# The first head of a fused attention block by halves from two queues, with the second head's work in another order

## The chip, the cores and the metric

The kernel runs on one core of one Trainium2 chip. The metric is the device time of one execution in microseconds (us). The core has five engines with a queue of instructions each: TensorE (PE, with weight loads shown apart as PEld), VectorE (DVE), ScalarE (ACT), GpSimd (POOL) and SyncE (SP, which issues most of the transfers). A transfer is issued by an engine's queue and carried out by 16 DMA engines.

## The reference, cut to what matters

Three layers follow one another: attention restricted to buckets, a gated layer, and a layer that mixes by Fourier transforms and ends in two matmuls. The change touches the start of the first.

```python
# batch 2, 8 heads, 768 positions, head size 64, 6 bits
q_bits = (q @ proj > 0); k_bits = (k @ proj > 0)          # proj: 64 x 6
mask = bucket(q_bits)[:, None] == bucket(k_bits)[None, :]
scores = where(mask, q @ k.T / 8, -1e9)
attn = softmax(scores);  x = attn @ v                     # heads side by side: 2 x 768 x 512
x = sigmoid(conv(x)) * (x @ w_val) @ w_out                # causal convolution of 5 taps
u = x + real(fft2(x));  out = u + relu(layernorm(u) @ w_ch1) @ w_ch2
```

## The kernel before

All products run as float32r matmuls on numbers cut in two: a high part (`ht`, a copy rounded on its way out) and a low part (`lt`, what is left). The attention goes over 8 pairs of heads (`p`), a head `j` in each pair, and 6 tiles of 128 queries in each head: 96 tiles `n`. The order of instructions on each engine is the order in which the program writes them.

For a head, q and k are loaded side by side into `rqk` (`load`, L321), transposed on TensorE so that head size lies on partitions (q on 0 to 63, k on 64 to 127), and copied out as `ht` (ScalarE) and `lt` (VectorE). The bits come from a matmul with proj (`project_alone`, L445) and a sign (`L504`, `L509` for the first head, `start_bits` L535 for the second). Scores are two matmuls deep (`scores`, L549): the operand tiles `qk` (`q2`, `k2`) hold in their first half high and low parts, and in their second half the bits on partitions 0 to 6 (with a large weight, so that different buckets drive a score out of the softmax), and more low and high parts on 64 to 127. For the very first head these tiles are filled by copies of ScalarE and GpSimd in `start` (L460); for every later head by six transfers of SP (`qk_place`, L407) and two for the bits (`bits_place`, L431).

A tile then runs through `clamp` (L568, VectorE: reads the scores, leaves `sd` and the row's extreme), `expo` (L575, ScalarE), transposes (`ptp`, L593), a high copy (L601, ScalarE), a low copy (L605, VectorE) and the product with v (L616, TensorE). In the loop over `n` the scores and the clamp of tile n+3 stand beside the transposes of tile n. One bank pair (`pss`) holds the scores of the loop, so the scores of a tile wait for the clamp of the tile before; the pool `pst` has two buffers and holds the transposes.

`start` runs before the loop: first head, its bits, scores of tiles 0 to 2, second head's transposes and parts. In the first turns of the loop come the second head's bits (L538, then `bits_scale` on GpSimd, L458, then `bits_place`), loads of the convolution weights (`cwr`, L747, whose first use is VectorE's L146 in turn 2), and the transposes of the second pair (`qk_transpose`, L392), for which `load(1, 0)` and `load(1, 1)` have been issued by `start`.

Until the first data are there, TensorE runs matmuls on zeros (`idle`, L353; `WARM` counts them).

Of the kernel before, what the change touches and what calls it, by code (L numbers as in the profile page):

```python
# [10 lines left out]
F32 = mybir.dt.float32  # L11
# [23 lines left out]
WARM = (18, 3, 4)  # L35
# [48 lines left out]
def col_table():  # L84

    c = np.zeros((P, 6), np.float32)
    c[:64, 0] = 1.0
    c[64:, 0] = KSCALE
    c[:, 2] = -1.0
    c[0, 2] = 1.0  # L90
    c[:, 3] = -8.0 * 896 * 2.0 ** 20
    c[:, 4] = -8.0 * 897 * 2.0 ** 20

    for j in (0, NR):
        c[j : j + NB, 1] = 1.0
        c[j : j + NB, 5] = -0.5
        c[j + NB, 5] = 1.0
        c[j + 32 : j + 32 + NB, 1] = -2.0 * BIG
        c[j + 32 : j + 32 + NB, 5] = BIG
        c[j + 32 + NB, 5] = 3.0 * BIG  # L100
    return c
# [3 lines left out]
def block_kernel(  # L105
# [6 lines left out]
    def f32(ap):  # L112
        return ap.bitcast(F32)
# [7 lines left out]
    warm = cpool.tile([P, 1], F32, name="warm")  # L121
    nc.vector.memset(warm, 0.0)

# [178 lines left out]
    def attention(es):  # L302
# [24 lines left out]

        def load_v(p):
# [13 lines left out]

        ph = ap1.tile([P, 2, P], F32R, name="ph")
# [5 lines left out]

        zeros = ap0.tile([P, R, QB], F32R, tag="pth", name="zeros")[:, 0, :]  # L350
        nc.gpsimd.memset(f32(zeros), 0.0)
# [30 lines left out]
        nc.gpsimd.tensor_scalar(pr[64:128, :], pr[64:128, :], -1.0, 0.0, op0=ALU.mult, op1=ALU.add)  # L382
        project_parts(0)
# [8 lines left out]
        def qk_transpose(p, j, a):  # L392
# [11 lines left out]
            nc.scalar.activation(ht, tp, AF.Copy, scale=col[:, 0:1])  # L404
            nc.vector.scalar_tensor_tensor(lt, tp, col[:, 0:1], f32(ht), op0=ALU.mult, op1=ALU.subtract)
# [54 lines left out]
        def start():  # L460
# [7 lines left out]
            def turned(j, tps):  # L468
                for a in range(2):
                    for r in range(3):  # L470
                        nc.tensor.transpose(
                            tps[a][:, r * P : (r + 1) * P], rqk[:, j, 3 * a + r].rearrange("p i d -> p (i d)"), ident
                        )

            def high(j, tps):
                for a in range(2):
                    nc.scalar.activation(halves(st[0]["ht", j])[a], tps[a], AF.Copy, scale=col[:, 0:1])

            def low(j, tps):
                for a in range(2):  # L480
                    nc.vector.scalar_tensor_tensor(
                        halves(st[0]["lt", j])[a], tps[a], col[:, 0:1], f32(halves(st[0]["ht", j])[a]),
                        op0=ALU.mult, op1=ALU.subtract,
                    )

            first = two_banks()
            turned(0, first)
            idle(WARM[1])
            high(0, first)
            low(0, first)  # L490
            q1, q2_ = slice(0, HS), slice(HS, S)
            nc.scalar.copy(k2[0][0:64, 0, :], h[64:128, :])
            pool_copy(k2[0][64:128, 0, :], h[64:128, :])
            nc.scalar.copy(q2[0][0:64, 0, q1], h[0:64, q1])
            nc.scalar.copy(q2[0][64:128, 1, q1], h[0:64, q1])
            pool_copy(k2[0][64:128, 1, :], l[64:128, :])
            pool_copy(q2[0][64:128, 0, q1], l[0:64, q1])
            whole = pst.tile([P, 2, 512], F32, tag="t", name="bp")
            for a in range(2):
                project_alone(0, a, whole[0:64, a, :HS])  # L500
            bits = st[0]["bits"] = ap1.tile([P, S], F32R, tag="bits", name="bits")
            ks, qs = slice(32, 32 + NR), slice(0, NR)
            for a in range(2):
                nc.vector.tensor_scalar(halves(bits)[a][ks], whole[ks, a, :HS], 0.0, None, op0=ALU.is_gt)  # L504
# [929 lines left out]
```

## Time and profile before

| | |
|---|---|
| time, median of 3 runs | 617.6 us (616.6 to 618.74) |
| the profiled execution | 618.49 us, its span 616.7 us |
| TensorE busy | 603.8 us (98% of the span) |
| VectorE busy | 444.7 us (72%) |
| ScalarE busy | 358.6 us (58%) |
| GpSimd busy | 269.1 us (44%) |
| transfers | 62.02 MB, 101 GB/s over the span |

The span runs from the first to the last recorded instruction; the execution's own time has 1.79 us around it. Busy TensorE is no measure of how near it is to its peak, since its matmuls overlap and their ends are modelled. Of the 616.7 us the attention takes the first 250 or so; the change lies in the first 20.

### The profile page before, as it was taken

How to read it: one execution, taken by the hardware profiler on the slowest of the kernel's cores; microseconds unless marked ns; L12 is line 12 of the kernel's file. 1: busy time of each engine (PE TensorE's matmuls, PEld its weight loads, DVE VectorE, ACT ScalarE, POOL GpSimd, SP SyncE). 2: the span in 40 equal slices, each digit the busy share in tenths (PEclk: the TensorE clock that was granted, in tenths of full speed). 3: DMA queues.
4: the chain of work that ended last, by engine and by line, in shares of the span. 5: the costliest groups of instructions: out<-in, count | busy, mean ns of one | idle time of the engine just before them, and what ended most of it. 6: DMA issues, size and time to landing. Idle time of an engine off the chain costs nothing.

```text
span 616.7 us, 10435 instructions
## 1 busy us (share of the span) xinstructions
PE 603.8 (98%) x3711; PEld 539.2 (87%) x3711; DVE 444.7 (72%) x850; ACT 358.6 (58%) x712; POOL 269.1 (44%) x303
## 2 busy tenths in 40 slices
PE   8999999999999999999999999999999999999997
PEld 6889999999899989998899988888888888888886
DVE  5999999999899998799769788888885411111113
ACT  5988899988899887844625355555665111111121
POOL 8252488877788898792350633233231000000000
PEclk9999999999999999999999999999999999999999
DMA  6957585857566640162110243443440200000002
GB/s 141 224 127 172 130 182 147 180 150 157 151 156 166 191 120 14 61 243 70 36 35 0 70 132 118 126 136 109 133 136 1 103 0 1 2 0 1 0 1 102
DMA packets 54957, 62.02 MB, mean 101 GB/s; under 512 B 29184, under 2 KB 42664, under 8 KB 54650
## 3 DMA queue, kind: packets, MB, share of 16 engines
q1 hardware_dynamic: 54170, 57.81, 35.6%
q0 software_dynamic: 432, 3.55, 1.5%
q8 instruction: 29, 0.48, 0.3%
q14 instruction: 22, 0.18, 0.1%
q10 hardware_dynamic: 304, 0.01, 0.0%
HBM read 36.73 MB, written 3.19 MB: 65 GB/s over the span
## 4 chain that ended last, share of the span: by engine, by line
PE 72%; DVE 14%; ACT 3%; DMA 3%; issue 3%; POOL 2%; SPq 2%; ACTq 0%; POOLq 0%; DVEq 0%
PE pf L1341 20%; PE acc L1351 20%; PE sp L557 7%; PE op L616 6%; PE ptp L593 5%; DVE sd L568 3%; PE ps L1158 3%; DVE ptl L605 3%; PE ps L222 3%; PE ps L1222 2%; DMA qk<-ht 2%; PE late L222 1%; PE early L222 1%; PE bp L443 1%; DMA xs<-xc 1%
## 5 line engine op out<-in xcount | busy, mean ns | idle before, releaser
L1351 PE MATMUL acc<-w,hid 128*128 128x512 f32 x576 | 137.7, 391 | 0.0
L1351 PEld LDWEIGHTS acc<-w,hid 128*128 128x128 f32 x576 | 105.8, 188 | 20.3
L1344 DVE SCALAR_TENSOR_TENSOR hid<-pf,hid 128x512 fp32r<-128x512 f32 (+1 forms) x62 | 33.4, 556 | 120.4 <-ACT hid L1343 120.4
L1341 PE MATMUL pf<-uth,w 128*128 128x512 f32 (+1 forms) x496 | 96.8, 337 | 0.1
L568 DVE TENSOR_SCALAR_CACHE_REDUCE sd<-sp 128x768 f32<-128x768 f32 x96 | 91.1, 950 | 7.7 <-PE sp L557 7.2
L605 DVE TENSOR_TENSOR ptl<-ptp,pth 128x768 fp32r<-128x768 f32 x96 | 91.5, 953 | 5.9 <-ACT pth L601 3.8
L1343 ACT ACTIVATE hid<-pf 128x512 fp32r<-128x512 f32 (+1 forms) x62 | 28.9, 488 | 115.0 <-PE pf L1341 115.0
L557 PE MATMUL sp<-qk 128*128 128x512 f32 (+1 forms) x384 | 91.4, 360 | 4.3 <-DVE sd L568 3.2
L1341 PEld LDWEIGHTS pf<-uth,w 128*128 128x128 f32 x496 | 79.8, 189 | 13.8 <-DVE hid L1344 1.4
L575 ACT ACTIVATE sd<-sd,nm 128x768 f32<-128x768 f32 x96 | 90.1, 939 | 1.5 <-DVE sd L568 1.5
L601 ACT CAST pth<-ptp 128x768 fp32r<-128x768 f32 x96 | 77.1, 803 | 17.7 <-PE ptp L693 8.9
L162 POOL TENSOR_TENSOR w<-cv 128x512 fp32r<-128x512 f32 x31 | 40.1, 1294 | 88.8 <-DVE cv L157 80.3
L593 PE MATMUL ptp<-ident,sd 128*128 128x128 f32 x576 | 78.5, 272 | 0.2 <-ACT sd L575 0.2
L616 PE MATMUL op<-pth,v 128*128 128x256 f32 x288 | 74.1, 283 | 1.6 <-ACT xc L629 1.6
L616 PE MATMUL op<-ptl,v 128*128 128x256 f32 x288 | 73.8, 286 | 0.0
L557 PEld LDWEIGHTS sp<-qk 128*128 128x128 f32 x384 | 58.2, 189 | 13.8 <-DVE sd L568 7.4
L593 PEld LDWEIGHTS ptp<-ident,sd 128*128 128x128 f32 x576 | 65.8, 140 | 1.1 <-ACT sd L575 0.5
L616 PEld LDWEIGHTS op<-pth,v 128*128 128x128 f32 x288 | 54.2, 188 | 6.6 <-ACT xc L629 2.7
L634 POOL TENSOR_TENSOR xm<-xc,xs 64x256 f32<-64x256 f32 x48 | 35.2, 733 | 56.4 <-DMA xs<-xc 39.0
L616 PEld LDWEIGHTS op<-ptl,v 128*128 128x128 f32 x288 | 54.2, 188 | 0.3
L1341 PE MATMUL pf<-utl,w 128*128 128x512 f32 (+1 forms) x248 | 53.1, 336 | 0.0
L149 ACT ACTIVATE cv<-cv,col 128x512 int32<-128x512 int32 x32 | 23.2, 725 | 41.5 <-DVE cv L146 41.5
(214 smaller groups left out, 998.4 us busy)
## 6 DMA issues: line engine op xcount, KB each, us to landing
raw<-in_moe_w_ch_dram SPq DMA_DIRECT2D x32, 512.0 KB
qk<-ht SPq DMA_DIRECT2D x60, 192.0 KB
qk<-lt SPq DMA_DIRECT2D x30, 192.0 KB
rqk<-in_q_dram SPq DMA_DIRECT2D x16, 192.0 KB
rqk<-in_k_dram SPq DMA_DIRECT2D x16, 192.0 KB
rv<-in_v_dram SPq DMA_DIRECT2D x8, 384.0 KB
out_dram<-o SPq DMA_DIRECT2D x12, 256.0 KB
xs<-xc SPq DMA_DIRECT2D x47, 64.0 KB
```

Source lines behind the costliest of these rows:

```text
L162: nc.gpsimd.tensor_tensor(dst()[1], fold(g.bitcast(F32)), fold(e.bitcast(F32)), op=ALU.mult)
L557: nc.tensor.matmul(sp[:, cs], q2[i][:, m, qi * P : (qi + 1) * P], k2[i][:, m, cs], start=m == order[0], stop=m == order[1])
L568: nc.vector.tensor_scalar(sd[n], sp, CLAMP, None, op0=ALU.min, op1=ALU.min, accum_out=st[p]["nm"][:, n % 12 : n % 12 + 1],)
L575: nc.scalar.activation(sd[n], sd[n], AF.Exp, bias=st[p]["nm"][:, i : i + 1], scale=-1.0, accum_out=st[p]["sums"][:, i : i + 1],)
L593: nc.tensor.transpose(tp[:, r // 3, c0 : c0 + P], sd[n][:, r * P : (r + 1) * P], ident)
L601: nc.scalar.copy(p_parts(n)[0], tp)
L605: nc.vector.tensor_tensor(lo, tp, f32(ho), op=ALU.subtract)
L616: nc.tensor.matmul(po[kb], v3[:, r, c0 : c0 + P], pt[kb][x][:, r, :], start=r == 0 and x == 0, stop=r == R - 1 and x == 1,)
L634: add[kb] = lambda: nc.gpsimd.tensor_tensor(st[p]["xm"][mr, blk * QB : (blk + 1) * QB], xc[mr, :], xs[mr, :], op=ALU.add)
L1341: nc.tensor.matmul(pf, w[:, c, :], x[:, c, cs], start=n == 0, stop=n == 3 * NC - 1)
L1344: nc.vector.scalar_tensor_tensor(hl[:, cs], pf, 0.0, f32(hh)[:, cs], op0=ALU.max, op1=ALU.subtract)
L1351: nc.tensor.matmul(acc, x[:, ts_], w, start=f == 0 and n == 0, stop=f == NF - 1 and n == 2)
```

## The change

Loads. The first head's q and k come in halves of three rows each, q by SP's queue and k by ScalarE's. The two copies of proj go one by each queue, behind the halves. Warm-up matmuls: 13 for 18. The scale of the high and low parts is no column of the loaded table `col` any more, but a tile that VectorE sets.

proj's parts for the first head (`ph`, `pl`, `plus`) are made by VectorE, but for `plus`; GpSimd made them before. The first head's transposes, high and low parts go by halves. k's bits are written by VectorE straight into the operand tile, with scale and offset in one instruction, and q's go through `bits` and a ScalarE instruction (before, it was the other way round); rows of the table are exchanged for that. q's operands are filled for the first 128 columns first, then for the others of that half, then for the second half. The second head's transposes use the two banks of the first head's, not a tile of `pst`; three tiles of `pst` are then in use in the opening (two for the first head's bits, one for the scores of tile 1). The second head's high copies stand ahead of the first exponentials on ScalarE, and its low parts behind the clamp of tile 1 on VectorE. SP places the second head and its bits ahead of `load(1, 1)`.

```diff
-WARM = (18, 3, 4)
+WARM = (13, 3, 4)
...
+    nc.vector.memset(turn_scale[:64], 1.0)
+    nc.vector.memset(turn_scale[64:], KSCALE)
...
+        def load_halves():
+
+            t = st[0]["rqk"] = ap4.tile([P, 2, R, 2, D], F32, tag="rqk", name="rqk", bufs=2)
+            for a in range(2):
+                rs = slice(3 * a, 3 * a + 3)
+                for i, (eng, src) in enumerate(((nc.sync, q), (nc.scalar, k))):
+                    eng.dma_start(t[:, 0, rs, i, :], src[0, 0].rearrange("(p r) d -> p r d", r=R)[:, rs, :])
...
-        load(0, 0)
+        load_halves()
 
         pr = ap1.tile([P, NB], F32, name="pr")
-        for r in (0, 64):
-            nc.scalar.dma_start(pr[r : r + 64, :], proj)
+        nc.scalar.dma_start(pr[0:64, :], proj)
+        nc.sync.dma_start(pr[64:128, :], proj)
         nc.scalar.dma_start(col, t_col)
         load(0, 1)
...
-        nc.gpsimd.tensor_scalar(pr[64:128, :], pr[64:128, :], -1.0, 0.0, op0=ALU.mult, op1=ALU.add)
-        project_parts(0)
+        nc.vector.tensor_scalar(pr[64:128, :], pr[64:128, :], -1.0, None, op0=ALU.mult)
+        spots = [(slice(64 * x, 64 * x + 64), 32 * x) for x in range(2)]
+        for rs, c0 in spots:
+            nc.vector.tensor_copy(ph[rs, 0, c0 : c0 + NB], pr[rs, :])
+        for rs, c0 in spots:
+            hd = f32(ph)[rs, 0, c0 : c0 + NB]
+            nc.vector.tensor_tensor(ph[rs, 0, 64 + c0 : 64 + c0 + NB], hd, pr[rs, :], op=ALU.subtract)
+            nc.gpsimd.tensor_tensor(plus[rs, 0, c0 : c0 + NB], pr[rs, :], hd, op=ALU.subtract)
+        for rs, c0 in spots:
+            nc.vector.tensor_copy(pl[rs, 0, c0 : c0 + NB], f32(ph)[rs, 0, c0 : c0 + NB])
...
+            for a in range(2):
+                turned(0, banks_[a], a)
             idle(WARM[1])
+            for a in range(2):
+                high(0, banks_[a], a)
+                low(0, banks_[a], a)
+                pool_copy(halves(k2_[64:128, 0, :])[a], halves(h[64:128, :])[a])
+            tile0 = slice(0, P)
+            nc.scalar.copy(k2_[0:64, 0, :], h[64:128, :])
+            nc.scalar.copy(q2_[0:64, 0, tile0], h[0:64, tile0])
+            nc.scalar.copy(q2_[64:128, 1, tile0], h[0:64, tile0])
+            pool_copy(q2_[64:128, 0, tile0], l[0:64, tile0])
+            pool_copy(k2_[64:128, 1, :], l[64:128, :])
+            bps = [pst.tile([P, 2, 512], F32, tag="t", name="bp")[:, 0, :HS] for _ in range(2)]
...
+            k_bits(0)
+            q_bits(0, 0, P)
+            k_bits(1)
+            q_bits(0, P, HS)
+            second = two_banks()
             load_v(0)
             load(1, 0)
+            for a in range(2):
+                turned(1, second[a], a)
             idle(WARM[2])
+            high(1, second[0], 0)
+            q_scaled(0, P)
+            high(1, second[1], 1)
+            sp = [scores(0, order=(0, 1))]
+            q_scaled(P, HS)
+            q_rest(P, HS)
+            clamp(0, sp[0])
+            q_bits(1, 0, HS)
+            sp.append(scores(1, pst.tile([P, 2, 512], F32, tag="t", name="sp")))
+            expo(0)
+            clamp(1, sp[1])
+            q_scaled(HS, S)
+            for a in range(2):
+                low(1, second[a], a)
+            q_rest(HS, S)
             project_parts(1)
-            sp = [scores(0, order=(0, 1)), scores(1, pst.tile([P, 2, 512], F32, tag="t", name="sp"))]
-            clamp(0, sp[0])
-            expo(0)
-            low(1, second)
-            clamp(1, sp[1])
             sp = scores(2)
+            qk_place(0, 1)
             values(0, 0)
-            qk_place(0, 1)
-            load(1, 1)
             expo(1)
             clamp(2, sp)
...
             bits_scale(bits)
             bits_place(0, 1)
+            load(1, 1)
```

On VectorE, from the first low parts to the fourth clamp, stood before (`lt` low parts, `bits` and `qk` the bits, `sd` a clamp):

```order
L481 SCALAR_TENSOR_TENSOR lt<-bp,col,ht 128x384 x2
L504 TENSOR_SCALAR bits<-bp 7x384 x2
L509 TENSOR_SCALAR qk<-bp,col 7x384 x2
L568 TENSOR_SCALAR sd,nm<-sp 128x768
L481 SCALAR_TENSOR_TENSOR lt<-tp,col,ht 128x384 x2
L568 TENSOR_SCALAR sd,nm<-sp 128x768 x2
L538 TENSOR_SCALAR bits<-bp 64x384 x2
L568 TENSOR_SCALAR sd,nm<-sp 128x768
```

The same stretch of VectorE's queue in the changed kernel, begun three rows earlier so that the last of proj's small operations are seen:

```order
L396 TENSOR_TENSOR ph<-ph,pr 64x6 x2
L399 CAST pl<-ph 64x6 x2
L492 SCALAR_TENSOR_TENSOR lt<-bp,turn_scale,ht 128x384 x2
L519 TENSOR_SCALAR qk<-bp,col 7x384
L524 TENSOR_SCALAR bits<-bp 7x128
L519 TENSOR_SCALAR qk<-bp,col 7x384
L524 TENSOR_SCALAR bits<-bp 7x256
L604 TENSOR_SCALAR sd,nm<-sp 128x768
L524 TENSOR_SCALAR bits<-bp 7x384
L604 TENSOR_SCALAR sd,nm<-sp 128x768
L492 SCALAR_TENSOR_TENSOR lt<-bp,turn_scale,ht 128x384 x2
L604 TENSOR_SCALAR sd,nm<-sp 128x768
```

proj's operations stand ahead of the first low parts, the bits are in five pieces of which one stands between the clamps of tiles 0 and 1, and the second head's low parts moved from ahead of tile 1's clamp to behind it.

On ScalarE, from the first high copies to the second exponential, stood before (`ht` high copies, `qk` copies into the operand tiles and the scaling of bits, `sd` the exponentials):

```order
L477 ACTIVATE ht<-bp,col 128x384 x2
L492 CAST qk<-ht 64x768
L494 CAST qk<-ht 64x384
L495 CAST qk<-ht 64x384
L505 ACTIVATE qk<-bits,col 7x768
L477 ACTIVATE ht<-tp,col 128x384 x2
L575 ACTIVATE sd,sums<-sd,nm 128x768 x2
```

and stands now:

```order
L489 ACTIVATE ht<-bp,turn_scale 128x384 x2
L507 CAST qk<-ht 64x768
L508 CAST qk<-ht 64x128
L509 CAST qk<-ht 64x128
L489 ACTIVATE ht<-bp,turn_scale 128x384
L529 ACTIVATE qk<-bits,col 7x128
L489 ACTIVATE ht<-bp,turn_scale 128x384
L529 ACTIVATE qk<-bits,col 7x256
L611 ACTIVATE sd,sums<-sd,nm 128x768
L529 ACTIVATE qk<-bits,col 7x384
```

The second head's high copies moved in between the pieces of the scaling, ahead of the first exponential.

On SP, from the last placement of the second head to the loads of the loop's first turn, stood before (numbers tell tiles apart; `rqk_211` is the second pair's q and k):

```order
L416 DMA qk_155<-lt_172 64x768
L326 DMA rqk_211<-in_q_dram 128x6x64
L326 DMA rqk_211<-in_k_dram 128x6x64
L435 DMA qk_153<-bits_202 7x768
L435 DMA qk_155<-bits_202 7x768
L747 DMA cwr_299<-in_moe_conv_w_dram 20x128
L775 DMA wvr_301<-in_moe_w_val_dram 128x256
```

and stands now (the second pair's tile is `rqk_213` there):

```order
L432 DMA qk_155<-lt_172 64x768
L451 DMA qk_153<-bits_204 7x768
L451 DMA qk_155<-bits_204 7x768
L327 DMA rqk_213<-in_q_dram 128x6x64
L327 DMA rqk_213<-in_k_dram 128x6x64
L783 DMA cwr_308<-in_moe_conv_w_dram 20x128
L811 DMA wvr_310<-in_moe_w_val_dram 128x256
```

The load of the second pair's second head changed places with the bits; `cwr` stands behind it in both.

## Rows read from the trace of the kernel before

**Rows 1.** Busy time by stage: span of stretch, engines' busy us, PEclk, DMA, GB/s.

```profile
40.00:100.00 60.00, 59.17 (x445) 55.55 (x445) 57.19 (x109) 53.75 (x111) 32.74 (x39) 1.00 0.67 158
```

**Rows 2.** The same view of VectorE alone, from 21.2 to 37.2.

```profile
21.20:37.20 16.00, 15.73 (x35) 1.00 0.72 169
```

**Rows 3.** The chain that ended last, to 40 us: start, us, what.

```profile
9.46 1.14 DVE qk L509 x2
...
10.60 0.63 PE sp L557 x2
...
11.25 0.98 DVE sd L568 x2
...
16.08 0.98 DVE sd L568 x2
...
17.10 0.98 PE sp L557 x4
```

**Rows 4.** Timeline to 17 us: start, us, engine, line, what, idle time before it.

```profile
2.63 1.28 ACT L341 ACT_TABLE_LOAD   x1 [2.63 <-issue]
...
4.68 0.21 POOL L382 TENSOR_SCALAR pr<-pr 64x6 f32<-64x6 f32 x1 [0.30 <-DMA pr<-in_proj_dram]
...
5.58 0.64 PEld L471 LDWEIGHTS bp<-ident,rqk 128*128 128x128 f32 x6 [0.20 <-issue]
...
6.16 1.05 ACT L477 ACTIVATE ht<-bp,col 128x384 fp32r<-128x384 f32 x2 [2.04 <-PE bp L471]
...
7.25 0.83 ACT L492 CAST qk<-ht 64x768 fp32r<-64x768 f32 x1
...
8.63 0.51 ACT L495 CAST qk<-ht 64x384 fp32r<-64x384 f32 x1
...
9.52 1.03 ACT L505 ACTIVATE qk<-bits,col 7x768 fp32r<-7x768 f32 x1 [0.38 <-DVE bits L504]
...
12.13 1.14 DVE L481 SCALAR_TENSOR_TENSOR lt<-tp,col,ht 128x384 fp32r<-128x384 f32 x2
...
13.19 0.95 DVE L568 TENSOR_SCALAR_CACHE_REDUCE sd<-sp 128x768 f32<-128x768 f32 x1
...
14.94 1.01 DVE L538 TENSOR_SCALAR bits<-bp 64x384 fp32r<-64x384 f32 x2
...
16.12 0.97 POOL L458 TENSOR_SCALAR bits<-bits,col 64x768 fp32r<-64x768 f32 x1 [0.72 <-ACT pth L601]
```

**Rows 5.** The same view of SP's queue, issues to 20 us.

```profile
0.76 0.69 SPq L326 DMA_DIRECT2D rqk<-in_q_dram  x1
...
15.54 0.86 SPq L326 DMA_DIRECT2D rqk<-in_q_dram  x1
...
17.24 1.72 SPq L435 DMA_DIRECT2D qk<-bits  x2
19.00 0.45 SPq L747 DMA_DIRECT2D cwr<-in_moe_conv_w_dram  x1
```

**Rows 6.** DMA queues from 2 to 4.3 us: packets, MB, share of 16 engines.

```profile
q1 hardware_dynamic: 1595, 0.40, 77.0%
```

**Rows 7.** Busy time by stage in the opening; columns as in rows 1.

```profile
2.40:3.00 0.60, 0.60 (x5) 0.60 (x5) 0.00 (x0) 0.37 (x1) 0.60 (x2) 1.00 0.54 126
3.00:3.60 0.60, 0.60 (x5) 0.60 (x5) 0.00 (x0) 0.60 (x1) 0.60 (x2) 1.00 1.13 241
```

**Rows 8.** Timeline from 22 to 24 us; columns as in rows 4.

```profile
22.65 0.20 DVE L146 TENSOR_SCALAR conv_tmp<-cwr 20x128 int32<-20x128 int32 x1
...
23.31 0.49 PE L399 MATMUL tp<-ident,rqk 128*128 128x128 f32 x3
```

**Rows 9.** DMA queues from 12 to 20.1 us; columns as in rows 6.

```profile
q1 hardware_dynamic: 2069, 1.62, 95.0%
```

**Rows 10.** The tile of the warm-up matmuls, 1.7 to 4.8: ns min, median, max.

```profile
L356 PEld LDWEIGHTS idle<-zeros x15: 286/330/333, 1.7 to 4.7; 128*128 128x128 f32 x15
```

**Rows 11.** The same tile from 5.05 to 9.6 us.

```profile
L356 PEld LDWEIGHTS idle<-zeros x10: 188/190/267, 4.9 to 9.1; 128*128 128x128 f32 x10
```

More of the change, by code (lines that the diff above doesn't have):

```diff
@@ L86, in col_table @@
     c = np.zeros((P, 6), np.float32)
-    c[:64, 0] = 1.0
-    c[64:, 0] = KSCALE
     c[:, 2] = -1.0
@@ L466, in start @@
             h, l = f32(st[0]["ht", 0]), f32(st[0]["lt", 0])
[L468 to L487, printed above, removed]
-            idle(WARM[1])
[L489 to L498, printed above, removed]
-            for a in range(2):
-                project_alone(0, a, whole[0:64, a, :HS])
+            def turned(j, tp, a):
+                for r in range(3):
+                    nc.tensor.transpose(tp[:, r * P : (r + 1) * P], rqk[:, j, 3 * a + r].rearrange("p i d -> p (i d)"), ident)
@@ new lines, in high, with low @@
+            def high(j, tp, a):
+                nc.scalar.activation(halves(st[0]["ht", j])[a], tp, AF.Copy, scale=turn_scale)
+            def low(j, tp, a):
+                nc.vector.scalar_tensor_tensor(
+                    halves(st[0]["lt", j])[a], tp, turn_scale, f32(halves(st[0]["ht", j])[a]),
+                    op0=ALU.mult, op1=ALU.subtract,
+                )
+            q2_, k2_ = q2[0], k2[0]
+            banks_ = two_banks()
+            for a in range(2):
+                turned(0, banks_[a], a)
@@ L501, in start @@
+            pool_copy(k2_[64:128, 1, :], l[64:128, :])
+            bps = [pst.tile([P, 2, 512], F32, tag="t", name="bp")[:, 0, :HS] for _ in range(2)]
+            for a in range(2):
+                project_alone(0, a, bps[a][0:64])
             bits = st[0]["bits"] = ap1.tile([P, S], F32R, tag="bits", name="bits")
             ks, qs = slice(32, 32 + NR), slice(0, NR)
-            for a in range(2):
-                nc.vector.tensor_scalar(halves(bits)[a][ks], whole[ks, a, :HS], 0.0, None, op0=ALU.is_gt)
@@ L505, in start, with k_bits @@
-            nc.scalar.activation(
-                k2[0][0:NR, 1, :], f32(bits)[ks], AF.Identity, scale=col[ks, 1:2], bias=col[ks, 5:6]
-            )
-            for a in range(2):
+            def k_bits(a):
                 nc.vector.tensor_scalar(
-                    halves(q2[0][0:NR, 1, :])[a], whole[qs, a, :HS], 0.0, col[qs, 5:6], op0=ALU.is_gt, op1=ALU.add
+                    halves(k2_[0:NR, 1, :])[a], bps[a][ks], 0.0, col[ks, 5:6], op0=ALU.is_gt, op1=ALU.add
                 )
-            second = pst.tile([P, 2, 512], F32, tag="t", name="tp")
@@ L513, in start, with q_bits, q_scaled, q_rest @@
-            second = [second[:, a, :HS] for a in range(2)]
+            def q_bits(a, c0, c1):
+                nc.vector.tensor_scalar(
+                    bits[qs, a * HS + c0 : a * HS + c1], bps[a][qs, c0:c1], 0.0, None, op0=ALU.is_gt
+                )
+            def q_scaled(c0, c1):
+                nc.scalar.activation(
+                    q2_[0:NR, 1, c0:c1], f32(bits)[qs, c0:c1], AF.Identity, scale=col[qs, 1:2], bias=col[qs, 5:6]
+                )
+            def q_rest(c0, c1):
+                pool_copy(q2_[0:64, 0, c0:c1], h[0:64, c0:c1])
+                pool_copy(q2_[64:128, 0, c0:c1], l[0:64, c0:c1])
+                pool_copy(q2_[64:128, 1, c0:c1], h[0:64, c0:c1])
```

30 lines of the change are left out of this document (13 added, 17 removed).

## The prediction

> **What bounds the kernel now.** I read the busy times by stage first, then the chain of waits, then the timeline of the stretch that the change touches, then the DMA queues. Over the attention TensorE is what the work waits for: in the 60 us from 40 it is busy 59.17 [rows 1]. Before that, VectorE is: from 21.2 to 37.2 it is busy 15.73 of 16 us [rows 2]. Nothing of this work is changed. So the change can move the start of the steady work and no more: what it wins or loses by 37 us is carried to the end, and the reader must follow the first 23 us.
>
> In them one chain counts [rows 3, 4]. The first head's q and k land, TensorE transposes them at 5.58 after standing idle for 0.20 (the data ended that wait, not the warm-up matmuls ahead of it), ScalarE makes two high copies (from 6.16, 1.05), VectorE the low parts and then the bits, and the second half of the first scores starts when the q bits are there, at 10.60. The clamps of tiles 0 and 1 start at 11.25 and 13.19 (between them stand the second head's low parts, 1.14), the signs of the second head's bits at 14.94, and the clamp of tile 3 at 16.08. From there scores and clamps alternate.
>
> **The opening, step by step.** All times are of the one profiled execution (616.7 span, 618.49 its own time, which lies 0.9 above the median of 617.6).
>
> Landing. The first head's 0.39 MB are issued from 0.76 [rows 5], 0.40 MB are through by 4.3 [rows 6] and used at 5.58, so use follows 1.3 us behind the last bytes. The changed kernel moves the same bytes for this head by two queues, in halves; the first half (0.2 MB) is through near 3.5 at the rates of rows 7, usable near 4.8, the second near 5.5 as before. ScalarE now issues four DMAs before its table load (1.28 long, begun at 2.63 before) instead of three, so about 0.7 later, to some 4.7: just in time. Three transposes, not six, remain behind the second half: half of 0.64 [rows 4] saved, and the two high copies no longer stand behind one another. The second high copy ends near 6.5, not 7.2.
>
> At the start the rate was 126 GB/s for 0.6 us and 241 just after [rows 7], so a second issuing engine could save up to (241-126) x 0.6 = 69 KB, or 0.3 us. The Trainium skill says in DMA: Bandwidth & Descriptors, section Rules for kernel authors, that spreading DMAs over the issuing engines doesn't raise bandwidth and only saves issue time. By the rule the second half lands as k did; by the rows it could land 0.3 earlier, and the sum below would be 0.3 better. I take no saving, because the head's bytes are not all that the next steps wait for (proj comes behind them).
>
> ScalarE's path: k's copy 0.83, two copies of 128 columns (0.83 for 768 and 0.51 for 384 give about 0.30 each by the slope), the second head's first high copy (0.53; its transposes stand behind the projections on TensorE, to about 8.2), the scaling of 128 q bits (1.03 for 768, by the same slope about 0.4): 6.5 + 0.83 + 0.6, then 8.2 + 0.6 + 0.4 = 9.2.
>
> VectorE's path: the projection's parts move here from GpSimd and stand ahead of the low parts, so both low parts now wait for proj. Its two DMAs went first on their queue and were used at 4.68 [rows 4]; now each stands third, behind the head's halves, and I put it at 5.6, where those bytes are used. Seven small operations follow. The nearest row is 0.20 for 20x128 [rows 8]; successive operations overlap, so between 0.12 and 0.20 each, 0.85 to 1.4. Low parts 1.14 to 7.6 or 8.1, k bits, 128 q bits, k bits (1.14 for two of the first kind [rows 3], and 0.25) to 9.0 or 9.5. Both paths meet near 9.2: I take that, with 9.0 to 9.6 for the range. Before it was 10.60, so 1.4 won.
>
> Clamps. Tile 0's clamp follows after 0.65, at 9.85. Behind it the last q bits (0.5) and then tile 1's clamp, at 11.25; tile 1's scores need the second high copy and 256 scaled bits on ScalarE (9.2 to 10.3) and 0.98 of TensorE, so 11.3. That is 1.9 before 13.19. But the second head's low parts (1.06 from start to the next start) now stand between the clamps of tiles 1 and 2. The signs start at 11.3 + 1.06 + the 1.75 that the two clamps took = 14.1, against 14.94: 0.8 is won, and the order among clamps and low parts gave back the rest. Tile 3's clamp moves with it.
>
> GpSimd loses most of proj's small operations and gets three more copies of half a tile; the second head's parts of proj and v's parts follow as before. It scales the second head's bits (0.97) behind them, before at 16.12 after standing idle for 0.72 [rows 4]: that idle time is the cover, and I put the scaling at 15.2, right behind the signs. If the copies run 0.5 late, 0.5 is added to all that follows on SP.
>
> **What the moved load costs.** On SP the bits now go before the load of the second pair's second head. Before, bits were issued at 17.24, behind that load at 15.54, and 1.62 MB (six placements, the load, the bits) were through at 20.1 [rows 5, 9]. Now the bits are issued from 16.3 into a queue that has run dry and take 1.72 to issue; the load follows at 18.05 to 19.6, 2.5 later than before, and behind it conv_w (cwr), at 19.6 instead of 19.00. Two readers wait for these. The transposes of that load (L399 at 23.31) would now like to run near 22.5, and VectorE's first step on cwr (L146 at 22.65) near 21.85 [rows 8]. In the opening a load of this size took 3.5 us from issue to its last bytes and 4.8 to use. From 18.05 that is 21.6 and 22.9, and cwr stands right behind. So VectorE waits between 0 and 1.0 us, in front of a clamp that everything behind it needs. I take 0.5, since this load runs in an empty queue where the opening's had four more behind it, and TensorE's transposes are then just in time. What is left is 0.8 - 0.5 = 0.3.
>
> The rest I cost at nothing: the five warm-up matmuls left out ran while TensorE had nothing else; new scale constants are set by VectorE while it waits for data; the second head's transposes use two other banks, which are free once the low parts have read them; the projection of the second head now waits for its low parts to leave those banks, but it has until 14.1.
>
> Sum: span 616.7 - 0.3 = 616.4, that execution 618.2, the median 617.6 - 0.3 = 617.3. With every bound at its better end (landing 0.3, no wait on cwr) 1.1 is won, with every one at its worse end 0.6 is lost.
>
> **Rivals.**
> First, the gain comes through whole: cwr and the load land within 3.8 us of 18.05 and VectorE never waits. 617.6 - 0.8 = 616.8, or 616.5 with the earlier landing. For it speaks the empty queue; against it, that the bytes alone took 3.5 us in the opening.
>
> Second, more is won than I count, because small VectorE operations are cheap, proj lands before the second half, and ScalarE's copies come earlier: tile 1's clamp can't start before 10.6 then, and with no wait on cwr 1.5 to 1.9 is won: 616.1 to 615.7.
>
> Third, it ends slower, by TensorE's clock. In the rows the warm-up's weight loads took 330 ns until 4.7 and 190 from 5.05 [rows 10, 11], which is the step from 1.2 to 2.4 GHz, though the granted clock stands at 1.00 from the start [rows 7]. TensorE had been busy without a pause since 1.72. Now it is busy from about 1.3 to 4.1 and then pauses for each half. If the clock then rises only once the scores run, what lies on the path doubles: three transposes 0.3, the last projection 0.2, the second half of scores 0 0.3, scores 1 0.5 to 1.0: 1.3 to 1.8 us, of which the 0.3 is paid first. The time would be 618.6 to 619.1. It decides from the point at which the first projection's weight loads run at the slower pace. The Trainium skill has it in TensorE: Matmul & The Clock Gate, section Part 1, that the slower clock is the default and sustained activity releases it; this trace agrees in that the first loads were the slow ones. Against the rival: the pauses are short, and 13 cold matmuls come before them, where 14 sufficed to bring the step before [rows 10].
>
> Fourth, the opening doesn't come earlier: proj lands after 6.2 and the seven operations take 1.4, so 9.2 becomes 10.0 and all is eaten by the wait on cwr: 617.6 to 618.1.
>
> **How the numbers follow.** My forecast 0.42, first rival 0.23, second 0.12, clock 0.10, fourth 0.13. The predicted time is the forecast's, 617.3. The range goes from 615.8 (part of the second rival, and a median that scatters by some 0.5) to 618.5 (the fourth and the lower part of the third). The runs before lie from 616.6 to 618.74, so a change under 0.3% (1.85 us) can't be told from none: faster than 615.75 is most of the second rival's lower half and what scatter adds from the first, 0.16; slower than 619.45 is the worst of the third with scatter, 0.06; the rest, 0.78, lies within.
>
> **What would show it.** In the profile after: the first transposes start near 4.8 and the second three near 5.5; VectorE's first low part waits for its own small operations, and these for proj; the second half of scores 0 starts near 9.2, the clamps of tiles 0 and 1 near 9.85 and 11.3, the signs near 14.1; bits leave SP near 16.3 and the load near 18; the first VectorE step on cwr starts near 22.35 with an idle time of about 0.5 ahead of it, released by a DMA. No such idle time there makes the first rival right, slow weight loads after 6 us the third. A difference that arises behind 40 us, or one above 2 us, makes the prediction wrong in its reasons.

## The result, and the profile after

The changed kernel took 622.44 us (median of 10 runs, 619.31 to 625.91), the kernel before on the same chip 617.78 (10 runs, 616.19 to 618.74). The ratio is 1.0068, with a 95% interval of 1.0047 to 1.0089: slower by 4.2 us, where 617.3 and a range to 618.5 had been forecast. (Here and below the ratio is not the quotient of the two medians.) The profiled execution took 622.89, its span 621.1, which is 4.4 more than before.

Where it was lost can be read by lining up the same steps of the two profiled executions. The clamp of tile 3 starts at 16.02, before at 16.08 [rows 3]: the opening has won 0.06. The clamp of tile 6 starts at 24.57, before at 22.80: 1.77 late, all of it lost between two clamps, those of tiles 5 and 6. The clamp of tile 6 in the kernel before:

```profile
22.80 0.96 DVE L568 TENSOR_SCALAR_CACHE_REDUCE sd<-sp 128x768 f32<-128x768 f32 x1
```

From there to the end of the attention 0.9 more is lost, in steps up and down, and in the last stage, up to the span's end, 1.6.

The chain of waits that ended last, of the changed kernel (start, us, what), runs through the moved load:

```profile
15.93 0.97 POOL bits L474
...
17.39 0.40 SPq L451
...
18.63 0.62 SPq L327
...
19.30 0.65 SPq L327
...
19.99 4.41 DMA cwr<-in_moe_conv_w_dram
...
24.43 0.04 DVE conv_tmp L147
```

GpSimd scales the bits, SP issues them and only then the load of the second pair's second head, and `cwr` stands behind it and lands at 24.40. The timeline of the same stretch shows who stood there:

```profile
24.36 0.52 PE L415 MATMUL tp<-ident,rqk 128*128 128x128 f32 x3 [1.11 <-DMA rqk<-in_k_dram]
24.43 0.21 DVE L147 TENSOR_SCALAR conv_tmp<-cwr 20x128 int32<-20x128 int32 x1 [1.75 <-DMA cwr<-in_moe_conv_w_dram]
24.57 0.94 DVE L604 TENSOR_SCALAR_CACHE_REDUCE sd<-sp 128x768 f32<-128x768 f32 x1
```

VectorE stood idle for 1.75 before its first step on `cwr`, where before it came to that step at 22.65 without a wait [rows 8], and TensorE for 1.11 before the transposes of the load. The clamp behind it is the one that is 1.77 late.

The opening, from the same timeline:

```profile
4.24 1.23 PEld L486 LDWEIGHTS bp<-ident,rqk 128*128 128x128 f32 x6
...
4.94 0.17 DVE L390 TENSOR_SCALAR pr<-pr 64x6 f32<-64x6 f32 x1 [2.86 <-DMA pr<-in_proj_dram]
...
5.26 1.23 ACT L489 ACTIVATE ht<-bp,turn_scale 128x384 fp32r<-128x384 f32 x2 [0.49 <-PE bp L486]
5.32 0.36 DVE L393 CAST ph<-pr 64x6 fp32r<-64x6 f32 x2 [0.20 <-DMA pr<-in_proj_dram]
...
6.07 0.60 DVE L399 CAST pl<-ph 64x6 fp32r<-64x6 f32 x2
...
6.70 1.14 DVE L492 SCALAR_TENSOR_TENSOR lt<-bp,turn_scale,ht 128x384 fp32r<-128x384 f32 x2
...
8.65 0.58 ACT L489 ACTIVATE ht<-bp,turn_scale 128x384 fp32r<-128x384 f32 x1 [0.67 <-PE bp L486]
...
9.13 0.48 ACT L529 ACTIVATE qk<-bits,col 7x128 fp32r<-7x128 f32 x1
...
9.57 0.94 PE L593 MATMUL sp<-qk 128*128 128x512 f32 x4
...
10.55 0.96 DVE L604 TENSOR_SCALAR_CACHE_REDUCE sd<-sp 128x768 f32<-128x768 f32 x1 [0.70 <-PE sp L593]
...
11.90 0.93 DVE L604 TENSOR_SCALAR_CACHE_REDUCE sd<-sp 128x768 f32<-128x768 f32 x1
...
12.88 1.14 DVE L492 SCALAR_TENSOR_TENSOR lt<-bp,turn_scale,ht 128x384 fp32r<-128x384 f32 x2
...
13.94 0.95 DVE L604 TENSOR_SCALAR_CACHE_REDUCE sd<-sp 128x768 f32<-128x768 f32 x1
...
14.81 1.01 DVE L573 TENSOR_SCALAR bits<-bp 64x384 fp32r<-64x384 f32 x2
...
16.02 0.96 DVE L604 TENSOR_SCALAR_CACHE_REDUCE sd<-sp 128x768 f32<-128x768 f32 x1 [0.20 <-PE sp L593]
```

The reader is to see three things. The first head's transposes start 1.3 earlier than before (4.24 against 5.58 [rows 4]) but their six weight loads take 1.23 instead of 0.64. VectorE's low parts start at 6.70, hardly earlier than before (6.78): proj's small operations fill 4.94 to 6.67, while the high copies end at 6.49. And the clamp of tile 0 starts 0.70 earlier than before, tile 1's 1.29, tile 2's 0.12: what was won is given back by the second head's low parts, which now stand at 12.88 between two clamps.

The last stage was no part of the forecast. All 62 copies of one of its lines, first and last start, stand here of the kernel before and of the changed one (line, engine, what, count: ns min/median/max, first to last start):

```profile
L1343 ACT ACTIVATE hid<-pf x62: 373/486/597, 346.9 to 604.8; 128x512 fp32r<-128x512 f32 x31, 128x256 fp32r<-128x256 f32 x31
```

```profile
L1379 ACT ACTIVATE hid<-pf x62: 374/488/600, 349.7 to 608.9; 128x512 fp32r<-128x512 f32 x31, 128x256 fp32r<-128x256 f32 x31
```

257.9 us lie between first and last before, 259.2 after, though no instruction of that stage was changed.

### The profile page after: what moved, and what is told of

The parts are those of the page before. It is cut to its first block, busy times and chain, and to the rows that moved or that the text cites. A ratio compares the mean times of both kernels' runs of the same rounds, so it can differ in the third digit from the quotient of the medians.

```text
span 621.1 us, 10441 instructions
## 1 busy us (share of the span) xinstructions
PE 605.9 (98%) x3706; PEld 538.8 (87%) x3706; DVE 446.5 (72%) x861; ACT 359.4 (58%) x714; POOL 269.4 (43%) x299
## 4 chain that ended last, share of the span: by engine, by line
PE 65%; DVE 13%; DMA 6%; POOL 6%; ACT 3%; issue 2%; SPq 1%; POOLq 0%; ACTq 0%; DVEq 0%
PE pf L1377 20%; PE acc L1387 20%; PE sp L593 4%; PE op L652 4%; PE ptp L629 3%; PE ps L1194 3%; DMA xs<-xc 3%; DVE sd L604 3%; DVE ptl L641 3%; PE ps L223 3%; DMA qk<-ht 3%; PE ps L1258 2%; POOL xm L670 1%; PE late L223 1%; PE early L223 1%
```

## The experiments

Theory A: several things cost, each by itself: at first the load behind the bits (order) and the scale's new tile, which moves every tile allocated after it by 32 bytes (shift); after the first two groups of runs also a lower clock of TensorE in some runs. The rivals put it on one of them, or on the new opening as a whole.

### The shift taken out

The scale lies in the padding of the tile beside it, so that no other tile is moved.

```diff
-    warm = cpool.tile([P, 1], F32, name="warm")
-    turn_scale = cpool.tile([P, 1], F32, name="turn_scale")
+    warm_ = cpool.tile([P, 2], F32, name="warm")
+    warm, turn_scale = warm_[:, 0:1], warm_[:, 1:2]
```

> The changed kernel with its new scale tile put into the padding of the small tile `warm`, so that no later tile moves by 32 bytes. Theory A (two causes: the load of the second pair and conv_w land late and stop VectorE for 1.8 us near 24 us; and the new tile moves every later tile of the left side by 32 bytes, which slows the last stage by about 0.06 us in each of its iterations): the stop near 24 us stays, the last stage takes 259.2 us again in place of 260.5, and the time falls by 1.3 us to about 621.1. Rival B (the last stage is slower for another reason, as the clock or another chip): the time stays at 622.4.

618.23 us, ratio 1.0016 (0.9997 to 1.0034). The last stage went back to its old length:

```profile
L1379 ACT ACTIVATE hid<-pf x62: 374/486/597, 348.8 to 606.7; 128x512 fp32r<-128x512 f32 x31, 128x256 fp32r<-128x256 f32 x31
```

257.9 again. The late clamp of tile 6 stayed (1.69 behind before). The median fell by 4.2, where theory A had 1.3 and rival B nothing: the stage explains a part of it, and the rest comes up again under the sum below.

### The old order of the load in the changed kernel

```diff
             qk_place(0, 1)
+            load(1, 1)
             values(0, 0)
...
             bits_place(0, 1)
-            load(1, 1)
```

> The changed kernel with the load of the second pair's second head issued ahead of the second head's bits again, as in the kernel before; all else is kept. Theory A: no stop of VectorE on conv_w, the clamp of tile 6 starts near 22.8 and not at 24.57, the time falls by 1.8 us to about 620.6. Rival C (the loss comes from the opening's order, and a stop near 24 us would come at any rate): the clamp of tile 6 stays behind 24 us and the time at 622.4.

619.09 us, ratio 1.0020 (1.0001 to 1.0039); theory A had 620.6. The wait is gone, the long last stage (259.1) is not:

```profile
22.02 0.20 DVE L147 TENSOR_SCALAR conv_tmp<-cwr 20x128 int32<-20x128 int32 x1
...
22.15 0.94 DVE L604 TENSOR_SCALAR_CACHE_REDUCE sd<-sp 128x768 f32<-128x768 f32 x1
```

```profile
L1379 ACT ACTIVATE hid<-pf x62: 373/486/599, 345.5 to 604.6; 128x512 fp32r<-128x512 f32 x31, 128x256 fp32r<-128x256 f32 x31
```

The clamp of tile 6 starts 0.65 before that of the kernel before, and that is what its tile 3 had won (0.63): nothing is lost between them. Up to tile 3 the computing engines have the instructions of the changed kernel, whose profiled execution won 0.06; VectorE's timeline in this one:

```profile
4.62 0.17 DVE L390 TENSOR_SCALAR pr<-pr 64x6 f32<-64x6 f32 x1 [2.53 <-DMA pr<-in_proj_dram]
...
5.70 0.34 DVE L399 CAST pl<-ph 64x6 fp32r<-64x6 f32 x2
...
9.98 0.96 DVE L604 TENSOR_SCALAR_CACHE_REDUCE sd<-sp 128x768 f32<-128x768 f32 x1 [0.75 <-PE sp L593]
...
15.45 0.96 DVE L604 TENSOR_SCALAR_CACHE_REDUCE sd<-sp 128x768 f32<-128x768 f32 x1 [0.20 <-PE sp L593]
```

### Each of the two alone, added to the kernel before

The shift, by a tile of 4 bytes that nothing uses; and the order, by the load behind the bits:

```diff
+    cpool.tile([P, 1], F32, name="pad")
```

```diff
             qk_place(0, 1)
-            load(1, 1)
...
             bits_place(0, 1)
+            load(1, 1)
```

> The kernel before with one unused tile of 4 bytes after `warm`, which moves every later tile of the left side by 32 bytes; nothing else. Theory A: attention as before, the last stage 1.3 us longer, 617.8 + 1.3 = 619.1. Rival B: 617.8.

> The kernel before with the second head's bits issued ahead of the load of the second pair's second head; nothing else. Theory A: the load is issued near 19.0 and lands near 24.5, TensorE's transposes of it and VectorE's step on conv_w wait for it, the clamp of tile 6 or 7 starts 1.5 to 2 us later, 617.8 + 1.8 = 619.6. Rival C: 617.8, since bits that land earlier make up for it.

The unused tile: 618.72 us, ratio 1.0010 (0.9995 to 1.0025). The timing can't tell that from nothing; the last stage of its profiled execution can. Its rows, then two rows of TensorE's timeline there, of the kernel before and of this one:

```profile
L1344 ACT ACTIVATE hid<-pf x62: 374/486/599, 346.8 to 605.9; 128x512 fp32r<-128x512 f32 x31, 128x256 fp32r<-128x256 f32 x31
```

```profile
526.08 1.98 PE L1341 MATMUL pf<-uth,w 128*128 128x512 f32 x8
527.89 1.07 PE L1341 MATMUL pf<-utl,w 128*128 128x512 f32 x4
```

```profile
526.57 2.03 PE L1342 MATMUL pf<-uth,w 128*128 128x512 f32 x8
528.44 1.09 PE L1342 MATMUL pf<-utl,w 128*128 128x512 f32 x4
```

259.1 us for the stage, 1.2 more than before. Eight matmuls of 512 columns take 527.89 - 526.08 = 1.81 before (226 ns each) and 1.87 here (234). With 31 rounds of 12 such matmuls that is 31 x 12 x 7.5 ns = 2.8 us; those of 256 columns go the other way (medians 120 and 117 ns from start to start), which gives 31 x 12 x 3 ns = 1.1 back: 1.7 by these, 1.2 by the rows. (The medians overstate it: over the whole stage the mean from start to start rises by some 4 ns for 512 columns and falls by 1 for 256, and 31 x 12 x 3 ns is 1.1.)

The order: 619.89 us, ratio 1.0024 (1.0008 to 1.0039), and the same wait as in the changed kernel, in a kernel that has nothing else of the change:

```profile
24.14 0.22 DVE L146 TENSOR_SCALAR conv_tmp<-cwr 20x128 int32<-20x128 int32 x1 [1.59 <-DMA cwr<-in_moe_conv_w_dram]
```

So both cost by themselves; the order is shown in the time as well, the shift in the profile. There it holds for every execution profiled for this document: the nine whose tiles lie where they did before take 257.8 or 257.9 for the stage, the five with the shift in either direction (the next experiment has the other one) 259.1 to 259.4.

### Shift the other way

The zeros' tile lies in the column table's padding, so that the tiles lie 32 bytes lower than before.

```diff
-    col = cpool.tile([P, 6], F32, name="col")
+    col_ = cpool.tile([P, 7], F32, name="col")
+    col, warm = col_[:, 0:6], col_[:, 6:7]
...
-    warm = cpool.tile([P, 1], F32, name="warm")
```

> The kernel before with the one-column tile of zeros put into the padding of the column table, so that every tile of the left side lies 32 bytes lower than before (the changed kernel lies 32 higher). Theory A1 (what counts is an odd or even number of 32 bytes): the matmuls of the last layer go to about 234 and 117 ns from start to start, the last stage is 1.2 to 1.6 us longer, the time 618.5 to 619. Theory A2 (only the addresses of the shift upward are bad): 227 ns stay, the last stage is the same within 0.4, the time 617.3 to 618.

620.04 us, ratio 1.0024 (1.0006 to 1.0041); the stage takes 259.4:

```profile
L1343 ACT ACTIVATE hid<-pf x62: 373/488/600, 344.6 to 604.0; 128x512 fp32r<-128x512 f32 x31, 128x256 fp32r<-128x256 f32 x31
```

```profile
524.59 2.03 PE L1341 MATMUL pf<-uth,w 128*128 128x512 f32 x8
526.46 1.10 PE L1341 MATMUL pf<-utl,w 128*128 128x512 f32 x4
```

(526.46 - 524.59) / 8 = 234 ns, as with the shift upward. That is theory A1: 32 bytes cost in either direction. Which of the two operands, or which pair of addresses, decides was not tried.

### Both taken out, and the load earlier still

Without shift and with the old order; and without shift and with the load right behind `load(1, 0)` in the opening, where the queue had time to spare:

```diff
             load(1, 0)
+            load(1, 1)
             for a in range(2):
...
             bits_place(0, 1)
-            load(1, 1)
```

> The changed kernel with both supposed causes taken out: the scale tile in the padding of `warm`, and the load of the second pair's second head ahead of the bits. Theory A (the two causes add up, and the opening itself is a small gain): tile 6's clamp 0.6 earlier than in the kernel before, the last stage as long as there, time 617.85 - 0.6 to - 1.2 = about 616.9. Rival D (the causes hide behind one another, or the opening costs something later): 618.2 or more.

> As a_both, but the load of the second pair's second head is issued in the opening right behind that of the first head, where SP has nothing to do for some 4 us. Theory A: no reader of that load or of conv_w waits, bits land early too, tile 6's clamp 0.7 to 1.0 earlier than before, about 616.8. Rival D: the load's 0.39 MB collide with the second head's placements, the scores of tile 6 wait for those, and the time is 618 or more.

Both taken out: 619.40 us, ratio 1.0030 (1.0010 to 1.0051). A was wrong here: 616.9 had been expected. The profiled execution has neither the wait nor the long stage (tile 6 is 0.12 ahead of before, the stage takes 257.8), and still the time was not better than before; 1.3 us of its profiled execution were lost on before between tiles 40 and 80, which the edits don't touch. Rival D (618.2 or more) has the number; what its loss is made of follows in part with the clock. The earlier load: 618.06, ratio 1.0015 (0.9996 to 1.0034). SP issues its second half, k, at 7.13, and `cwr` right behind the bits:

```profile
7.13 1.05 SPq L327 DMA_DIRECT2D rqk<-in_k_dram  x1
...
18.56 0.45 SPq L783 DMA_DIRECT2D cwr<-in_moe_conv_w_dram  x1
```

No wait is left at tile 6, so the collision of rival D isn't there, though the time is the one it gave; tile 6 is 0.16 ahead of before, where theory A had 0.7 to 1.0. The Trainium skill, DMA: Bandwidth & Descriptors, section Rules for kernel authors, says to issue a transfer early and to wait on it late. This trace agrees: here 15.9 us ahead (7.13 to 23.01) left no wait, and 5.1 (19.30 to 24.36 in the changed kernel) were 1.1 too few.

What the two have in common are runs in which the mean granted clock of TensorE was 0.997 or lower: 4 of 12 in each. In the earlier load's runs these took 620.39 to 621.27, the other eight 616.37 to 619.32. The changed kernel has 4 such runs in 10 (622.43 to 625.91, the other six 619.31 to 622.89). Of the 105 runs of the kernel before that have their clock on record 2 were such, and 1 of 12 with the order alone. Without these runs the median is 617.25 with the earlier load and 618.27 with both taken out, against 617.14 before: the clock explains nearly all of the first difference and half of the second.

### The warm-up

What changed beside order and shift are the halves and the five warm-up matmuls left out. First the earlier load again, with 18 for 13:

```diff
-WARM = (13, 3, 4)
+WARM = (18, 3, 4)
```

> As a_early with 18 warm-up matmuls for 13, as the kernel before had. Theory A (proj's small operations on VectorE, not TensorE's clock or its transposes, set the low parts' start): first transposes start 1.07 us later, the low parts near the same time as in a_early (within 0.3), time within 0.3 us of a_early. Rival E (the slow clock is what keeps the opening's gain small): weight loads of the first transposes take 140 ns for 230, low parts and first clamp 0.3 to 0.6 earlier than in a_early.

616.76 us, ratio 0.9993 (0.9977 to 1.0009), no run of 12 with the lower clock. In the opening this is theory A (low parts at 6.54 against 6.63 with 13, tile 0's clamp 0.08 earlier), but the time is 1.3 better, which it had not: the gain lies in the runs and not in the opening. Then that line alone in the changed kernel, and its reverse in the kernel before:

> The changed kernel with 18 warm-up matmuls for its 13 and nothing else. Theory A (three separate causes: the load behind the bits about 1.7 us, the tiles moved by 32 bytes about 1.4 us, a lower granted clock in some runs because of the five matmuls left out): at most 1 of 12 runs has a mean granted clock below 0.998 (the changed kernel 4 of 10), the second head's first weight loads take about 140 ns each again, the median falls from 622.4 to 620.2 to 621.2, and the span keeps the step of about 1.7 at the sixth tile and 1.3 in the last stage. Rival R (the low clock comes from the new opening's pauses, not from the warm-up's length): 3 or more of 12 runs stay low and the median stays at 621.8 to 623.

> The kernel before with 13 warm-up matmuls for its 18 and nothing else. Theory A (the five matmuls set the clock): 3 to 5 of 12 runs have a mean granted clock below 0.998 and are about 3 us longer than the others, the others stay at 617.5, the median is 617.6 to 618.6. Rival R (the new opening brings the low clock): at most 1 of 12 runs is low, median 617.3 to 618.

The changed kernel with 18: 619.74 us, ratio 1.0026 (1.0010 to 1.0042), no run of 12 with the lower clock. So 2.7 of the 4.7 us between the medians hang on that one number, and rival R falls. But the kernel before with 13: 618.66, ratio 1.0008 (0.9988 to 1.0027), and no such run either. Theory A, that the five matmuls alone do it, is not borne out: by these runs it takes both, the halves and the short warm-up. (At 18 in 70, the share found below, 12 runs would show none about 3 times in 100.) In the profile of the kernel before with 13 TensorE's weight loads are these:

```profile
1.72 2.85 PEld L356 LDWEIGHTS idle<-zeros 128*128 128x128 f32 x13 [1.72 <-POOL zeros L351]
5.67 0.64 PEld L471 LDWEIGHTS bp<-ident,rqk 128*128 128x128 f32 x6 [1.11 <-issue]
```

and with 18 in the changed kernel:

```profile
1.45 3.84 PEld L364 LDWEIGHTS idle<-zeros 128*128 128x128 f32 x18 [1.45 <-DVE zeros L353]
5.24 0.69 PEld L486 LDWEIGHTS bp<-ident,rqk 128*128 128x128 f32 x6
```

In both the transposes come after 5 us and run at the pace of 2.4 GHz (0.64 and 0.69 for six loads); in the changed kernel they come at 4.24 and take 1.23, nearly all at half that pace, though the column of the granted clock has 1.00 there too. How long the slow pace lasts there differs between executions: in the changed kernel's, the first projection's weight load took 0.13 at 5.96; in three others with the same opening (shift out, both out, earlier load) it was still slow:

```profile
6.10 0.22 PEld L464 LDWEIGHTS bp<-ht,ph 128*64 128x64 f32 x1
```

Over all kernels with the halves (those of the next experiment too), 18 of 70 runs with 13 warm-up matmuls had the lower clock and 0 of 36 with 18. Where in such a run the clock is lost stays open: no profiled execution is one of them (their mean clocks are 0.999 and 1.000). In size, 0.003 to 0.005 less over 620 us is 1.9 to 3.1 us of the full clock; the runs with it are 2.4 to 5.9 longer than the others of their kernel, by the medians, so a rest is left that this doesn't explain.

### proj ahead of the halves

From the earlier load, proj's two transfers go first on their queues, with 13 warm-up matmuls and with 18:

```diff
-        load_halves()
-
         pr = ap1.tile([P, NB], F32, name="pr")
         nc.scalar.dma_start(pr[0:64, :], proj)
         nc.sync.dma_start(pr[64:128, :], proj)
+        load_halves()
```

> As a_early with proj's two DMAs issued ahead of the first head's halves on both queues. Theory A (proj gates the low parts): proj's first operation on VectorE starts near 3.5 and not at 4.6 to 4.9, the low parts start with the high copies near 5.9 and not at 6.1 to 6.7, the first clamp 0.3 to 0.7 earlier, time 0.3 to 0.7 below a_early. Rival F (the halves, now 0.6 later, gate instead): first clamp no earlier, time as a_early.

> The changed kernel with the scale in the padding of the zeros' tile, the second pair's second head loaded right behind its first, proj's two loads ahead of the halves, and 18 warm-up matmuls. Theory A: no run or 1 of 12 with a clock below 0.998, the fourth clamp 0.6 to 0.8 earlier than in the kernel before, median 616.0 to 616.6, ratio 0.998. Rival (proj's early landing wins nothing that is kept): like the version without it, 616.8, ratio 0.999 to 1.000.

With 13: 617.61 us, ratio 1.0015 (0.9990 to 1.0040), 2 of 12 runs with the lower clock (622.07 and 624.32). With 18: 617.43, ratio 0.9989 (0.9975 to 1.0003), none. VectorE's timeline with 13, then with 18:

```profile
2.69 0.79 DVE L389 TENSOR_SCALAR pr<-pr 64x6 f32<-64x6 f32 x1 [0.60 <-DMA pr<-in_proj_dram]
...
5.82 1.36 DVE L491 SCALAR_TENSOR_TENSOR lt<-bp,warm,ht 128x384 fp32r<-128x384 f32 x2 [0.70 <-ACT ht L488]
...
9.87 0.96 DVE L603 TENSOR_SCALAR_CACHE_REDUCE sd<-sp 128x768 f32<-128x768 f32 x1 [0.67 <-PE sp L592]
```

```profile
6.73 1.14 DVE L491 SCALAR_TENSOR_TENSOR lt<-bp,warm,ht 128x384 fp32r<-128x384 f32 x2 [1.61 <-ACT ht L488]
...
10.56 0.96 DVE L603 TENSOR_SCALAR_CACHE_REDUCE sd<-sp 128x768 f32<-128x768 f32 x1 [0.68 <-PE sp L592]
```

With proj early and 13, low parts start at 5.82 and the clamp of tile 0 at 9.87; tile 3's clamp is 0.75 ahead of before: theory A, and rival F falls. With 18, VectorE waits 1.61 for the high copies, whose transposes stand behind the warm-up until 5.31, and tile 3's clamp is 0.05 ahead, where theory A had 0.6 to 0.8. So in these profiles the opening wins what was forecast only with the short warm-up, and with that some runs have the lower clock. Neither version is shown to beat the kernel before: the intervals of both reach over 1.

## Why the prediction was wrong

It forecast 0.3 us less and got 4.2 more. Four of its steps failed. In ratio, the warm-up matmuls left out, put at nothing, are worth 0.0042 (2.6 us); the moved load, put at 0.5 us, 0.0024 (1.5 us); the scale's tile, put at nothing, 0.0010 to 0.0024 (0.6 to 1.5 us). And the opening's gain, put at 0.8 at tile 3, was 0.06 in the profiled execution.

**The moved load: the wait that was sized too small.** The prediction put `cwr` "right behind" a load that is through by 21.6 and usable by 22.9, so that "VectorE waits between 0 and 1.0 us", and took 0.5. Measured were 1.75 in the changed kernel and 1.59 with this move alone. The load was issued at 18.63, not 18.05 (the signs were 0.7 late and GpSimd's own work on v ended at 15.87, so its scaling started at 15.93, not 15.2), and its transposes ran at 24.36, 5.7 us after issue began, where the opening's 4.8 had been taken for the upper end. One instance is no upper end. The queue was empty of earlier work, as argued, but not of later work: the convolution's weights, v and the next pair's q and k were issued from 20.61 on, before the load was used. From 18.6 to 24.4 us the queue moved (packets, MB, share of 16 engines)

```profile
q1 hardware_dynamic: 2092, 1.02, 71.1%
```

of which the load and `cwr` are 0.41 MB. So "an empty queue where the opening's had four more behind it" was no difference; whether the bytes behind it made the load longer was not tried. In ratio this step is worth 0.0024 (0.0008 to 0.0039), 1.5 us; the forecast's value was 0.5.

**The opening: right in its chain, wrong in two terms.** Forecast 0.8 at tile 3, measured 0.06 in the profiled execution. Everything behind tile 0's clamp went as worked out: 9.85, 11.3 and 14.1 for the two clamps and the signs became 10.55, 11.90 and 14.81, each 0.6 to 0.7 late. So all of the miss lies ahead of that clamp. Of it 0.4 is ScalarE: the second head's transposes ended 0.4 later than the 8.2 that was put for them, their high copy started at 8.65, the scaling of the first q bits ended at 9.61 instead of 9.2. The other 0.3 is TensorE: the clamp was put 0.65 behind the scores, as if half of them had run before, as they do in the kernel before [rows 3], but the second head's transposes and four warm-up matmuls now stand ahead of them and all four matmuls (0.94) run at 9.57. That proj's landing is what the chain hangs on was right: 5.6 had been put for it and 4.94 was measured, but its operations took 1.73 against the 1.4 allowed, and proj moved to the front gives 9.87 and 0.75, the forecast's 9.85 and 0.8. How much of the 0.8 comes differs between executions of the same opening: four profiled ones won 0.04 to 0.14 at tile 3, and the one with the old order of the load 0.63, with tile 0's clamp at 9.98. There proj was used at 4.62 and its operations took 1.42, within what was allowed; in the four it was used at 4.86 to 4.94, and the last two operations (`pl`) took 0.59 or 0.60 in place of 0.34. The two queues gave more than the nothing that the prediction took. The stretch from 2.4 to 3.6 us of the changed kernel (columns as in [rows 7]):

```profile
2.40:3.00 0.60, 0.60 (x5) 0.60 (x4) 0.00 (x0) 0.00 (x0) 0.60 (x2) 1.00 1.19 267
3.00:3.60 0.60, 0.60 (x5) 0.60 (x5) 0.00 (x0) 0.33 (x1) 0.60 (x2) 1.00 1.26 279
```

267 and 279 GB/s, before 126 and 241 [rows 7]. (267-126+279-241) x 0.6 = 107 KB more were moved in this stretch, at these rates 0.4 us. One queue reached 276 a little later (3.6 to 4.2), so the second engine brought the bytes forward and not the peak up. This agrees with the rule of the Trainium skill that the prediction cites (DMA: Bandwidth & Descriptors, section Rules for kernel authors), by which issuing from several engines saves issue time only.

**"The five warm-up matmuls left out ran while TensorE had nothing else."** Costed at nothing, because TensorE had nothing else to do; it is the largest term. With 18 of them the ratio falls from 1.0068 to 1.0026. The third rival, given 0.10, saw that the clock could be at stake, and priced it inside the opening, at 1.3 to 1.8 us. Inside the opening it cost little: six weight loads took 1.23 for 0.64, hidden behind proj's operations, and from 5.84 on the loads run in 188 to 192 ns. The rival's sign, slow weight loads after 6 us, is seen in three other executions with this opening, and they were no worse at tile 3. The price was paid by part of the runs as a whole, each 2.4 to 5.9 longer by the medians; at which point of them is not shown.

**"New scale constants are set by VectorE while it waits for data."** The instructions cost nothing; their tile did. It was counted as two instructions and not as 32 bytes in front of all that is allocated behind it: 1.2 to 1.6 us of the last stage in the profiles (the higher figures up to the span's end); in ratio 1.0010 (0.9995 to 1.0025) upward and 1.0024 (1.0006 to 1.0041) downward.

**The sum.** The opening without the other three costs is 0.9993, the order adds 0.0024 and the shift 0.0010 to 0.0024. That makes 1.0027 to 1.0041 against the 1.0026 (1.0010 to 1.0042) measured with 18 warm-up matmuls, which the intervals allow; the short warm-up takes it to 1.0068. The single removals from the changed kernel gave 1.0016, 1.0020 and 1.0026, together more than was lost. A part of this is the share of runs with the lower clock (4 of 10 in the changed kernel, 1 of 12 without shift, 3 of 12 with the old order); whether it varied by chance or for a reason these counts can't tell. It is not all: without those runs the medians are 620.27, 618.10 and 618.16, so that each of these two removals takes off 2.1 or more where the changed kernel is 2.5 behind before. Why they don't add stays open. The attention's later steps are open as well: between tiles 40 and 80 the profiled executions gain up to some 2.2 us on the kernel before or lose up to 1.9. The largest loss is that of the kernel before with 13 warm-up matmuls, so that such a step can't be put down to order, shift or halves.

## What to carry to other kernels

A wait bounded by one earlier instance is bounded from one side only: put the worse end beyond that instance (here 5.7 us came for 4.8), and look at what else is issued to the same queue before the data are used. A new small tile is an edit of every address behind it; put it into padding, or compare the matmuls' time from start to start in stages that were not touched. Taking out work that only keeps an engine busy can have a price, and a single profile may not show it: look at the granted clock of every run. And profile an opening more than once before its tenths are explained: the same one won 0.04 to 0.63 us here.

## What the runs showed of the hardware that was not expected

float32r matmuls of 512 columns went from 226 to 234 ns from start to start when the tiles of one side moved by 32 bytes, up or down, and those of 256 columns on `uth` from 120 to 117 (up) or 119 (down); the tiles `uth` and `utl` on the other side had not moved. Another line of the same stage, whose operands both moved (`acc`), kept its 227 ns.

A lower mean granted clock (0.995 to 0.997 for 0.998 to 1.000) came with 2.4 to 5.9 us more, by the medians of each kernel's runs, in 18 of 70 runs. What sets these 70 apart from the 36 without it is five matmuls on zeros in the first 6 of 620 us.

Seven operations of 64 partitions by 6 elements took 1.42 to 1.73 us on VectorE, one wait of 0.16 to 0.20 among them: some 0.2 each, a fifth of what one of 768 elements takes. The last two took 0.59 or 0.60 in the four executions in which GpSimd began a copy while they ran, at 6.03 to 6.12, and 0.34 or 0.35 in three in which all or nearly all of them was done by then (5.94 to 6.60).
